# An attention and expert kernel on one core: which engine runs two passes, and which queue loads the first group

## The chip, the core and the metric

The kernel runs on one core of a Trainium2 chip. A core has five engines with an instruction queue each, taken in order: TensorE (PE: matrix products and transposes, with its weight loads shown apart as PEld), VectorE (DVE), ScalarE (ACT), GpSimd (POOL) and SyncE (SP, which here only issues transfers). Transfers between the chip's main memory and the on-chip memory are issued by SP or ACT and run beside the engines. The metric is the device time of one execution in microseconds.

## What is computed

`x` has 4 batches of 11456 rows with 128 columns. Two steps follow one another, all in float32.

```python
def mab(q, kv):
    s = scale * (q @ kv.transpose(0, 2, 1))
    s = s - s.max(-1, keepdims=True)
    a = np.exp(s)
    a /= a.sum(-1, keepdims=True) + 1e-09
    return a @ kv
h = mab(I, x)                 # I: 32 inducing points, so h is 32 rows a batch
return mab(x, h)              # every row of x attends to those 32 rows
```

The result goes through a mixture of experts: a row with `x @ w_skip > 0` takes the best of 8 experts by `x @ w_gate`, and adds `gate * (relu(x @ w1[e]) @ w2[e])` to itself; the others stay as they are. Because every row after the attention is a mean of 32 rows of `h`, the kernel does the expert's work on those 32 rows once a batch, with the weights of one expert, and the gates row by row; a last part (`others`) checks whether any row would have needed another expert.

## The kernel before, in words

The host hands `x` over transposed, so a batch is a tile of 128 partitions (the columns of x) by 11456. A batch is cut into six **groups**: five of 2048 rows of x and one of 1216, which comes first in batch 0 and last in the others. A group is four **quarters** side by side, so that four products of 32 partitions fill the 128.

`first` (lines 348 to 438) handles a group's part in `h`: PE makes the scores (L361), DVE their maximum (L366, L371), ACT the exponentials (L375), PE transposes x and the exponentials (L400, L384), ACT or DVE copies these out of the accumulator banks (L324 or L326), PE sums (L410), DVE adds up (L419). `middle` closes a batch: `h`, the expert, its weights.

`second` (lines 637 to 824) handles a group's rows against `h`. PE makes scores (L659), DVE transposes them back into rows (L664) and finds each row's maximum (L666). Then come three passes of equal shape, each one two-input operation over the whole tile of 128 x 512 (128 x 320 in the short group): `less` subtracts the maximum (L670), `norm` multiplies by one over the sum (L682), and `scale2` multiplies by the row's gate (L786) into a tile `v`. Between them ACT takes the exponential (L673) and DVE sums (L677); DVE transposes the results of norm and of scale2 (both L687) for the closing products of PE (L837). `emit` copies those out (tile `o`) and stores them.

Nobody writes the order down. Each piece is an `Op` with the engines it may run on and a guessed cost on each (`pool(W)`, `dve(W)`, `act(W)`, lines 307 to 317). `in_order` (L65) plays the pieces through a small model of engines and buffers and gives each to the engine that it expects to be done first; `best_order` (L140) draws 1200 changes of the ranks from a fixed seed and keeps those that end no later by this model. A piece that may run on two engines has a `spare` of its own (L55), by which DVE is held back, and which is drawn again too (L162). So a change in what may run where alters every draw behind it, and with it the order of the whole program. The chosen pieces are then issued one after another; each engine runs its own in that order.

`load` (L330) brings a group's columns in. For the very first group (`k == 0`) the cut is at the quarters, so four transfers of 128 x 304; for the others it is in the middle. All are issued by SP. ACT issues two small transfers at the start: the inducing points (`iT_sb`, L219) and the gate weights (L222); and it scales `iT_sb` (L220).

Of the kernel before, what the change touches and what calls it, by code (L numbers as in the profile page):

```python
# [173 lines left out]
def kernel(  # L174
# [9 lines left out]
    nc = tc.nc  # L184
# [122 lines left out]
    def pe(w):  # L307
        return {"PE": 0.1 + 0.9 * w / 512}

    def dve(w):  # L310
        return {"DVE": 0.17 + 0.53 * w / 512}

    def act(w):
        return {"ACT": 0.22 + 0.37 * w / 512}

    def pool(w):
        return {"POOL": 0.1 + 0.95 * w / 512}
# [12 lines left out]
    def load(k, after):  # L330
        b, g = divmod(k, NG)
        s = bt[b]
        G = s.groups[g]
        st = Steps(k)
        buf = s.xbuf[g] = Buf("x")
        cut = G.s1[1:] if k == 0 else [GC // 2]
        cut = [0] + [c for c in cut if c < G.cols] + [G.cols]

        def go(o):
            t = s.x[g] = xp.tile([P, GC], F32, tag="x", name=f"x_{b}_{g}")  # L340
            for c, d in zip(cut, cut[1:]):
                nc.sync.dma_start(out=t[:, c:d], in_=xT[b, :, G.col0 + c:G.col0 + d])

        s.xin[g] = st.add({"SP": 0.08 * len(cut)}, go, after, take=[buf], size=G.cols * 0.512)
        return st
# [291 lines left out]
    def second(s, G, x, main):  # L637


        b, g = s.b, G.g  # L640
        W, nb, nh = G.w2, G.nb, G.nh
        st = {}
        keep = main is None
        L = Steps(b * NG + g + LEAD)
        bs, bl, be, blt = Buf("ps"), Buf("ps"), Buf("e"), Buf("lt")
# [4 lines left out]
        bex = Buf("ex")  # L650
# [33 lines left out]
        def back(k, src):  # L684
            if k == 2:
                st["u2"] = wk.tile([P, GC // Q], F32, tag="u2", bufs=BUFS["u2"], name=f"u2_{b}_{g}")
            nc.vector.transpose(out=st[f"u{k}"][:, 0:W], in_=st[src][:, 0:W])  # L687
# [100 lines left out]
        o = L.add(pe(W), scores, s.o_hc, last["s2"], take=[bs, be, st["b1"]], free=[s.xbuf[g]] if keep else [])  # L788
        last["s2"] = o if keep else None
        o = L.add({"DVE": 2 * dve(W)["DVE"]}, tokens, o, free=[bs])  # L790
        o = L.add({**pool(W), **dve(W)}, less, o)
        o = L.add(act(W), exps, o, take=[bex])
        o = L.add({"DVE": dve(W)["DVE"] + 0.28}, total, o)
        s.o_total.append(o)
        o_v = L.add({**pool(W), **dve(W)}, norm, o, free=[bex])
        st["o1"] = o = L.add(dve(W), lambda o: back(1, "e"), o_v)
        if keep and G.quarters:
            o = L.add({"PE": 0.35}, logits_q, o, s.o_lrq, take=[bl, blt])
            o_m = L.add({"DVE": 0.58}, relative_q, o, free=[bl])
            o_x = L.add({"ACT": 0.6}, gexp_q, o_m)  # L800
            o_c = L.add({"POOL": 1.06}, claim_q, o_m)
            s.o_claim.append(o_c)
            o = L.add({"DVE": 0.54}, gate_q, o_x)
            o = L.add({"POOL": 0.36}, pick_q, o, o_c)
            bm = Buf("ps")
            o = L.add({"PE": 0.35}, to_streams, o, take=[bm])
            o = L.add({"ACT": 0.24, "DVE": 0.17}, gates_in, o, free=[bm])
            o = L.add({**pool(W), **dve(W)}, scale2, o, take=[bv], free=[be, blt])
            st["o2"] = L.add(dve(W), lambda o: back(2, "v2"), o, take=[st["b2"]], free=[bv])
            return st, L  # L810
        o = L.add({"PE": 0.3 + 0.8 * W / 512}, logits, o, s.o_lr, take=[bl, blt])
        o_m = L.add({"DVE": dve(W / 2)["DVE"] + 0.29}, relative, o, free=[bl])
        o = L.add({"POOL": 0.4}, gless, o_m)
        o_x = L.add({"ACT": 0.31}, gexp, o)
        if keep:
            o_c = L.add({"POOL": 0.73}, claim, o_m)
            s.o_claim.append(o_c)
            o = L.add({"DVE": 0.55}, gate, o_x)
            o = L.add({"POOL": 0.2}, pick, o, o_c)
        else:  # L820
            o = L.add({"DVE": 2.0}, lambda o: main(st, lv, gv, two), o_x)
        o = L.add({**pool(W), **dve(W)}, scale2, o, take=[bv], free=[be, blt])
        st["o2"] = L.add(dve(W), lambda o: back(2, "v2"), o, take=[st["b2"]], free=[bv])
        return st, L

# [142 lines left out]
    def other_group(s, gr, w2s, sgn, code, same, G, col0):  # L968
# [5 lines left out]
        def gates(st, lv, gv, two):  # L974
# [22 lines left out]
            nc.vector.tensor_tensor(out=two(gm), in0=two(own), in1=two(sm), op=ALU.mult)  # L997

        st, steps = second(s, G, lambda: x, gates)
        for i, buf in enumerate(st["bufs"]):  # L1000
            buf.idx = i if buf.tag == "ps" else 0
# [20 lines left out]
    def all_steps():  # L1022
        ops = []
        starts = []
        for b, s in enumerate(bt):
            s.xbuf, s.xin, s.first_score = {}, {}, {}
            s.lastm = s.laste = s.lastd = None
            for g in range(NG):
                k = b * NG + g
                ops += load(k, starts[k - AHEAD] if k >= AHEAD else None)  # L1030
                ops += first(s, g)
                starts.append(s.first_score[g])
            ops += middle(s)
            for g, G in enumerate(s.groups):
                st, L = second(s, G, lambda s=s, g=g: s.x[g], None)
                emit(s, G, st, L)
                ops += L
            ops += marking(s, (b + 1) * NG + LEAD + 1)
        return ops + judge(B * NG + LEAD)
# [45 lines left out]
```

## Time and profile before

| | |
|---|---|
| median of 3 runs | 236.57 us (235.46 to 236.66) |
| the profiled execution | 235.9 us, its span from first to last instruction 234.0 us |
| PE, DVE, ACT, POOL busy | 205.8, 178.4, 141.9, 101.4 us |
| mean granted clock of TensorE | 0.966 |

A row of a group view names line, engine, operation, output and inputs, how often, then the busy time in us, the mean of one in ns, and the idle time of the engine before it with what ended it. A row of the view by stretches gives the stretch, its length, the busy time and count of PE, PEld, DVE, ACT and POOL, the granted clock, the share of the transfer engines and GB/s. A busy PE is not PE at its peak: ends of matmuls are modelled.

### The profile page before, as it was taken

Reading aid. Unit: us, or ns where it says so; the run is one execution under the profiler, and the core shown is the slowest. Engines: PE = TensorE matmul, PEld = TensorE weight load, DVE = VectorE, ACT = ScalarE, POOL = GpSimd, SP = SyncE. Lnnn points to the kernel's source line nnn. Section 1 sums busy time; section 2 is a strip of 40 time slices with the busy share of each in tenths; the row PEclk is TensorE's granted clock in tenths of the full one; section 3 lists DMA queues with packets and bytes.
Section 4 is the critical chain, followed back from the end, with each engine's and each line's share of the span. In section 5 each row is a group of like instructions: output and inputs, shape, how many; then the busy total and the mean of one; then the engine's idle time right before and its main releaser. Section 6 shows DMA issues by size and latency. Waiting matters only on the chain.

```text
span 234.0 us, 6690 instructions
## 1 busy us (share of the span) xinstructions
PE 205.8 (88%) x2541; PEld 117.7 (50%) x2542; DVE 178.4 (76%) x484; ACT 141.9 (61%) x326; POOL 101.4 (43%) x231
## 2 busy tenths in 40 slices
PE   4999999999899999998899999899998996869700
PEld 1667776675446754357534565564554332324400
DVE  3244256789888898799899887989998999998510
ACT  2377665655678867668657767477759462554710
POOL 6000000236468740137472162162788647988300
PEclk9999999999999999999999999999999999897975
DMA  6999960760898409995099957600405794161970
GB/s 176 372 418 408 407 235 2 279 263 3 294 347 296 179 4 291 354 417 202 3 349 274 368 197 233 235 3 1 182 4 209 257 372 172 44 263 54 388 265 10
DMA packets 16617, 51.66 MB, mean 221 GB/s; under 512 B 1984, under 2 KB 4928, under 8 KB 16576
## 3 DMA queue, kind: packets, MB, share of 16 engines
q1 hardware_dynamic: 16288, 51.12, 58.9%
q8 instruction: 22, 0.36, 0.6%
q14 instruction: 19, 0.16, 0.2%
q10 hardware_dynamic: 288, 0.02, 0.1%
HBM read 27.68 MB, written 23.46 MB: 219 GB/s over the span
## 4 chain that ended last, share of the span: by engine, by line
PE 55%; DVE 28%; POOL 5%; ACT 4%; issue 4%; DVEq 0%; ACTq 0%; POOLq 0%
PE bank L400 13%; PE bank L837 12%; PE bank L361 8%; PE bank L659 5%; PE bank L410 5%; DVE u L687 4%; PE bank L384 4%; DVE ts L666 3%; DVE ng L366 2%; DVE sums L677 2%; DVE e L664 2%; POOL v L786 1%; PE bank L696 1%; POOL e L682 1%; ACT o L324 1%
## 5 line engine op out<-in xcount | busy, mean ns | idle before, releaser
L324 ACT COPY o<-bank 128x512 f32<-128x512 f32 (+1 forms) x93 | 45.8, 570 | 21.4 <-PE bank L837 17.0
L324 ACT COPY xt<-bank 128x512 f32<-128x512 f32 (+1 forms) x79 | 43.4, 593 | 16.7 <-PE bank L400 16.6
L400 PE MATMUL bank<-ident,x 128*128 128x128 f32 (+1 forms) x368 | 51.6, 284 | 0.4 <-DVE lr L541 0.2
L400 PEld LDWEIGHTS bank<-ident,x 128*128 128x128 f32 (+1 forms) x368 | 40.4, 142 | 13.2 <-issue 3.3
L670 POOL TENSOR_TENSOR e<-e,ts 128x512 f32<-128x512 f32 (+1 forms) x21 | 21.0, 1002 | 58.4 <-DVE ts L666 57.9
L682 POOL TENSOR_TENSOR e<-texp,ts 128x512 f32<-128x512 f32 (+1 forms) x22 | 22.1, 1004 | 31.0 <-DVE ts L679 11.6
L837 PE MATMUL bank<-u,hr 32*128 32x512 f32 (+1 forms) x192 | 27.7, 649 | 1.5 <-ACT o L324 1.5
L410 PE MATMUL bank<-xt,a1T 128*32 128x129 f32 (+1 forms) x736 | 25.1, 275 | 0.3 <-ACT o L324 0.3
L361 PE MATMUL bank<-x,iT_sb 128*32 128x512 f32 (+1 forms) x192 | 25.4, 583 | 0.0
L366 DVE TENSOR_REDUCE ng<-bank 128x1 f32<-128x512 f32 (+1 forms) x24 | 15.3, 637 | 13.0 <-PE bank L361 12.2
L837 PE MATMUL bank<-u,yr 32*128 32x512 f32 (+1 forms) x192 | 24.6, 582 | 0.3 <-DVE u L687 0.3
L659 PE MATMUL bank<-x,hc 128*32 128x512 f32 (+1 forms) x192 | 23.6, 573 | 0.0
L786 POOL TENSOR_TENSOR v<-e,gs 128x512 f32<-128x512 f32 (+1 forms) x21 | 21.0, 1002 | 5.6 <-ACT gs L324 3.1
L410 PEld LDWEIGHTS bank<-xt,a1T 128*32 128x32 f32 (+1 forms) x736 | 19.5, 109 | 5.9 <-issue 2.2
L673 ACT ACTIVATE texp<-e 128x512 f32<-128x512 f32 (+1 forms) x24 | 14.7, 610 | 12.5 <-POOL e L670 8.7
L375 ACT ACTIVATE a<-bank,bias 128x512 f32<-128x512 f32 (+1 forms) x20 | 13.4, 670 | 10.7 <-DVE bias L371 8.7
L687 DVE STREAM_TRANSPOSE u<-e 128x512 f32<-128x512 f32 (+1 forms) x24 | 16.0, 666 | 1.4 <-POOL e L682 1.3
L384 PE MATMUL bank<-ident,a 128*128 128x128 f32 (+1 forms) x92 | 15.1, 286 | 1.6 <-DVE acc L419 1.3
L664 DVE STREAM_TRANSPOSE e<-bank 128x512 f32<-128x512 f32 (+1 forms) x24 | 15.8, 658 | 0.8 <-PE bank L659 0.8
L687 DVE STREAM_TRANSPOSE u<-v 128x512 f32<-128x512 f32 (+1 forms) x24 | 15.9, 665 | 0.7 <-POOL v L786 0.4
L666 DVE TENSOR_REDUCE ts<-e 128x16 f32<-128x512 f32 (+1 forms) x24 | 15.7, 653 | 0.8
L677 DVE TENSOR_REDUCE sums<-texp 128x16 f32<-128x528 f32 (+1 forms) x24 | 15.5, 646 | 0.7 <-ACT texp L673 0.7
(147 smaller groups left out, 280.2 us busy)
## 6 DMA issues: line engine op xcount, KB each, us to landing
x<-in_xT_dram SPq DMA_DIRECT2D x43, 512.0 KB, 7.8
out_dram<-o SPq DMA_DIRECT2D x40, 512.0 KB, 3.6
out_dram<-o SPq DMA_DIRECT2D x8, 304.0 KB, 3.4
w1s<-in_w_dram SPq DMA_DIRECT2D x4, 512.0 KB, 3.7
w2s<-in_w_dram SPq DMA_DIRECT2D x4, 512.0 KB, 5.5
x<-in_xT_dram SPq DMA_DIRECT2D x4, 152.0 KB, 3.1
x<-in_xT_dram SPq DMA_DIRECT2D x3, 96.0 KB, 5.7
iT_sb<-in_iT_dram ACTq DMA_DIRECT2D x1, 16.0 KB, 2.2
```

The source lines that it names most:

```text
L324: nc.scalar.copy(out=out, in_=in_)
L361: nc.tensor.matmul(ps[q * M:(q + 1) * M, 0:W], lhsT=iT_sb, rhs=s.x[g][:, G.s1[q]:G.s1[q] + W], start=True, stop=True)
L384: nc.tensor.transpose(out=pa[0:w, i * P:(i + 1) * P], in_=st["a"][:, c:c + w], identity=ident)
L400: nc.tensor.transpose(out=px[0:w, q * P:(q + 1) * P], in_=s.x[g][:, o:o + w], identity=ident)
L410: nc.tensor.matmul(ph[q * M:(q + 1) * M, 0:P + 1], lhsT=st["aT"][0:w, i, q * M:(q + 1) * M], rhs=xts[bx.idx][0:w, i, q, :], start=(i == 0) ...
L659: nc.tensor.matmul(ps[q * M:(q + 1) * M, 0:W], lhsT=s.hc[:, 0:M], rhs=x()[:, G.s2[q]:G.s2[q] + W], start=True, stop=True)
L666: nc.vector.tensor_reduce(out=mx[:, 0:nb], in_=blocks(t), axis=AX.X, op=ALU.max)
L670: on(o).tensor_tensor(out=blocks(t), in0=blocks(t), in1=wide(st["mx"]), op=ALU.subtract)
L682: on(o).tensor_tensor(out=blocks(st["e"]), in0=ev(M), in1=wide(st["i"]), op=ALU.mult)
L687: nc.vector.transpose(out=st[f"u{k}"][:, 0:W], in_=st[src][:, 0:W])
L786: on(o).tensor_tensor(out=blocks(u), in0=blocks(st["e"]), in1=wide(st["gm"]), op=ALU.mult)
L837: nc.tensor.matmul(bank(bp[q].idx)[:, 0:G.w1], lhsT=m[r, :], rhs=st[k][r, c], start=(k == "u1"), stop=(k == "u2"))
```

## The change

Of the three passes, `norm` and `scale2` may run on POOL alone; `less` still may run on POOL or DVE. The second and fourth quarter of the very first group are issued by ACT instead of SP.

```diff
 def load(k, after):
@@
-            for c, d in zip(cut, cut[1:]):
-                nc.sync.dma_start(out=t[:, c:d], in_=xT[b, :, G.col0 + c:G.col0 + d])
+            for i, (c, d) in enumerate(zip(cut, cut[1:])):
+                (nc.scalar if k == 0 and i % 2 else nc.sync).dma_start(out=t[:, c:d], in_=xT[b, :, G.col0 + c:G.col0 + d])
@@ def second(s, G, x, main):
-        o_v = L.add({**pool(W), **dve(W)}, norm, o, free=[bex])
+        o_v = L.add(pool(W), norm, o, free=[bex])
@@
-            o = L.add({**pool(W), **dve(W)}, scale2, o, take=[bv], free=[be, blt])
+            o = L.add(pool(W), scale2, o, take=[bv], free=[be, blt])
@@
-        o = L.add({**pool(W), **dve(W)}, scale2, o, take=[bv], free=[be, blt])
+        o = L.add(pool(W), scale2, o, take=[bv], free=[be, blt])
```

What the order of the instructions becomes is shown at three places.

The start on ACT (`x_0` is the first group's tile, `xt` and `a_0_0` are what first copies and computes of it); a row with + is new:

```order
 L220 ACT_TABLE_LOAD
 L220 ACTIVATE iT_sb<-iT_sb 128x32
+L342 DMA x_0_184<-in_xT_dram 128x304 x2
 L324 COPY xt_164<-bank_76 128x4x128
 L375 ACTIVATE a_0_0_198<-bank_77,ng_0_207 128x304
```

The two transfers stand behind the scaling of `iT_sb`, and on SP two of the four are gone ahead of the second group's. PE's and DVE's rows for this group are the same in both.

The middle, in batch 1 (`v_1_1` is scale2's output for the second group of batch 1, `gs` its gates). Before, on DVE:

```order
L371 TENSOR_TENSOR bias_5_1854<-ng_5_1852,bias_4_1627 128x1
L326 COPY gs_2_163<-bank_72 128x16
L326 COPY gs_0_153<-bank_76 128x16
L786 TENSOR_TENSOR v_1_1_1871<-e_1_1_1527,gs_0_153 128x512
L687 STREAM_TRANSPOSE u_1_1_1879<-v_1_1_1871 128x512
L460 TENSOR_REDUCE mn_1889<-bank_73 1x32
```

Now, on POOL:

```order
L772 TENSOR_TENSOR lt_5_1422<-lt_5_1422,gs_2_162 128x64
L772 TENSOR_TENSOR lt_1_1515<-lt_1_1515,gs_0_152 128x64
L786 TENSOR_TENSOR v_0_5_1593<-e_0_5_1132,gs_2_163 128x512
L786 TENSOR_TENSOR v_1_1_1617<-e_1_1_1372,gs_0_153 128x512
L760 TENSOR_SCALAR posm<-lt_0_1585 128x16
```

The pass has moved to POOL's queue, behind another group's, and stands earlier among the groups.

The end (`v_3_5` is the last group's scale2; `lo`, `lod`, `lon` and `marks` belong to the check for other experts). Before, on DVE:

```order
L895 TENSOR_REDUCE marks<-gxs 128x1
L786 TENSOR_TENSOR v_3_5_3200<-e_3_5_3007,gs_2_163 128x320
L687 STREAM_TRANSPOSE u_3_5_3203<-v_3_5_3200 128x320
L882 TENSOR_SCALAR lod_3208<-bank_71 128x1
L885 TENSOR_TENSOR lon_3210<-gmax,lod_3208 128x8
L886 TENSOR_TENSOR lon_3210<-lon_3210,gabs 128x8
L887 TENSOR_REDUCE marks<-lon_3210 128x1
L326 COPY o_5_0_3225<-bank_70 128x304
```

Now, on DVE:

```order
L895 TENSOR_REDUCE marks<-gxs 128x1
L882 TENSOR_SCALAR lod_3202<-bank_76 128x1
L885 TENSOR_TENSOR lon_3204<-gmax,lod_3202 128x8
L886 TENSOR_TENSOR lon_3204<-lon_3204,gabs 128x8
L887 TENSOR_REDUCE marks<-lon_3204 128x1
L687 STREAM_TRANSPOSE u_3_5_3209<-v_3_5_3200 128x320
L917 TENSOR_SCALAR two<-bank_76 128x8
```

The pass is gone to POOL, the transpose that reads it stands behind the check's steps, and the copy of the last output is ACT's.

Over the whole program DVE has the passes less, norm and scale2 three, two and three times before, and two, none and none now; of the 72, POOL has the rest.

## The prediction

> **What bounds the kernel now.** I read the page first, then the chain of waits, the stretches of the span, and the places that the change touches.
>
> ```profile
> span 234.0 us, 6690 instructions
> PE 205.8 (88%) x2541; PEld 117.7 (50%) x2542; DVE 178.4 (76%) x484; ACT 141.9 (61%) x326; POOL 101.4 (43%) x231
> PE 55%; DVE 28%; POOL 5%; ACT 4%; issue 4%; DVEq 0%; ACTq 0%; POOLq 0%
> ```
>
> The third line is the chain that ended last: TensorE holds 55% of it and VectorE (DVE) 28%. Where each holds it stands in the view by stretches (length; then PE, PEld, DVE, ACT, POOL busy):
>
> ```profile
> 10.00:30.00 20.00, 20.00 (x280) 14.33 (x279) 7.96 (x18) 12.63 (x28) 0.00 (x0) 1.00 1.03 411
> 82.00:99.00 17.00, 16.32 (x202) 8.19 (x202) 14.79 (x46) 11.94 (x28) 3.71 (x5) 1.00 0.65 213
> 99.00:126.00 27.00, 24.97 (x336) 14.26 (x331) 24.66 (x56) 17.58 (x40) 14.58 (x29) 1.00 0.66 246
> 160.00:180.00 20.00, 19.32 (x283) 10.64 (x279) 18.48 (x52) 15.18 (x40) 13.28 (x29) 1.00 0.25 99
> 190.00:210.00 20.00, 14.67 (x155) 5.75 (x154) 19.12 (x48) 9.08 (x20) 15.03 (x27) 0.91 0.49 192
> ```
>
> From 10 to 30 us PE never idles: whatever starts late there ends late. In the second to fourth stretch PE and DVE are both nearly full; PE idles 0.68, 2.03 and 0.68 us, 3.4 in all, and that is what a lighter DVE could give back there. From 190 on DVE holds the chain (19.12 of 20).
>
> **Part one: the first group's loads.** Rows of the start (start, duration; SPq and ACTq are the engines issuing a transfer):
>
> ```profile
> 0.77 0.41 SPq L342 DMA_DIRECT2D x<-in_xT_dram  x1
> 1.18 0.45 ACTq L222 DMA_DIRECT2D ws_sb<-in_ws_dram  x1
> 3.03 0.23 ACT L220 ACTIVATE iT_sb<-iT_sb 128x32 f32<-128x32 f32 x1
> 4.26 2.59 PE L361 MATMUL bank<-x,iT_sb 128*32 128x304 f32 x8
> 5.62 0.18 PEld L361 LDWEIGHTS bank<-x,iT_sb 128*32 128x32 f32 x2 [0.18 <-DMA x<-in_xT_dram]
> 6.78 2.82 PE L400 MATMUL bank<-ident,x 128*128 128x128 f32 x12
> ```
>
> Before, SP issues the four quarters back to back, and the fourth has landed when its weight load runs at 5.62. After, the second and fourth stand in ACT's order behind the scaling of iT_sb, which ends at 3.26: the order of the program, not the trace, puts them there. At 0.45 us an issue, the fourth leaves at about 3.7, while SP has begun on the big loads.
>
> ```profile
> x<-in_xT_dram SPq DMA_DIRECT2D x43, 512.0 KB, 7.8
> DMA to landing us min/median/max: 2.4/7.0/9.8
> 1.00:2.00 1.00, 0.39 (x1) 0.10 (x1) 0.47 (x1) 0.34 (x1) 0.96 (x12) 1.00 0.15 29
> 2.00:3.00 1.00, 0.00 (x0) 0.00 (x0) 1.00 (x1) 0.95 (x1) 1.00 (x6) 1.00 0.95 261
> 0.00:4.50 4.50, 1.36 (x5) 0.80 (x8) 2.10 (x3) 1.52 (x3) 3.84 (x38) 1.00 0.58 145
> 5.00:6.00 1.00, 1.00 (x5) 0.36 (x4) 0.00 (x0) 0.00 (x0) 0.00 (x0) 1.00 0.93 332
> ```
>
> The second line holds the twelve x loads issued up to 8 us. Lower bound: 2.4 us, the quickest, so 6.1, or +0.5. Upper bound: ACT's pieces wait as those behind SP's backlog do, 7.8 us, so 11.5, or +5.9. Between them, by sharing: by 4.5 us 145 x 4.5 = 652 KB had moved, which is the first group's 623 KB and the small loads; the last quarter was seen at 5.62, some 1.1 later. The loads issued at 0.77 had moved 29 KB by 2.0; at the next row's 261 GB/s that is 0.1 us of flow, so bytes start 1.1 us after issue, and ACT's start at 4.4. If the queues halve 332 GB/s, 311 KB take 1.9 us: landed at 7.4, +1.8. If the engines take a row from each in turn, ACT's rows of 304 x 4 = 1216 bytes against SP's 4096 get 23%, 76 GB/s: 4.1 us, landed at 9.6, +4.0. Both lie far nearer the lower bound than the upper; I take their middle, 8.5: **+2.9 us**.
>
> The second way is what the Trainium skill states (DMA: Bandwidth & Descriptors, section Queues, rings and completion order): the queues of SP and ACT run on the same 16 engines, and an engine with work on both switches between them packet by packet. By it the sum below would be 1.1 us longer, inside the first case's own range. No row of before shows two loaded queues.
>
> What hides it? Nothing: scores of the first group (L361) need all quarters, the transposes behind them (L400, 2.82 us) stand in the same order in both programs, ACT's copies and DVE's maximum wait for PE, and from 10 us on PE is full. Two x loads further on take the same turn-slot as the late quarters and issue later, but with megabytes queued ahead they cost nothing. What SP saves, 2 x 0.41 us of issue, brings the second group's data sooner; PE does not wait for it.
>
> **Part two: the passes.** Groups by shape (busy, mean ns):
>
> ```profile
> L786 POOL TENSOR_TENSOR v<-e,gs 128x512 f32<-128x512 f32 x18 | 18.9, 1048 | 5.4 <-ACT gs L324 3.1 <-DVE u L687 1.6 <-DVE gs L326 0.2
> L786 POOL TENSOR_TENSOR v<-e,gs 128x320 f32<-128x320 f32 x3 | 2.2, 725 | 0.2
> L786 DVE TENSOR_TENSOR v<-e,gs 128x512 f32<-128x512 f32 x2 | 3.0, 1485 | 0.0
> L786 DVE TENSOR_TENSOR v<-e,gs 128x320 f32<-128x320 f32 x1 | 0.5, 491 | 0.0
> L682 DVE TENSOR_TENSOR e<-texp,ts 128x512 f32<-128x512 f32 x1 | 0.7, 694 | 0.1
> L682 DVE TENSOR_TENSOR e<-texp,ts 128x320 f32<-128x320 f32 x1 | 0.5, 491 | 0.0
> L670 DVE TENSOR_TENSOR e<-e,ts 128x512 f32<-128x512 f32 x2 | 1.4, 692 | 0.1
> ```
>
> Eight of the 72 passes stood on DVE. After, norm (L682) and scale2 (L786) have none there and less (L670) has two, so six move net: DVE loses 2 x 1.485 + 0.491 + 0.694 + 0.491 + 0.692 = 5.3 us, and POOL gains 4 x 1.048 + 2 x 0.725 = 5.6, to some 107 of 234. The planner also ranks everything anew. On the chain of waits stood:
>
> ```profile
> 82.91 1.33 DVE v L786
> 100.97 0.69 DVE e L670
> 122.45 1.57 DVE v L786
> 162.16 0.70 DVE e L682
> ```
>
> That is 4.3 us at most, if nothing follows. But each dependent now waits 1.05 us for POOL, and PE has only 3.4 idle us in these stretches. I take half of the 2.03 us in the DVE-led stretch from 99 and 0.3 of the 0.68 from 160: **-1.3** (bounds -3.4 and 0).
>
> Why did the two cost 1.5 and not 0.69? Both engines' rows at that time:
>
> ```profile
> 122.42 1.05 POOL L786 TENSOR_TENSOR v<-e,gs 128x512 f32<-128x512 f32 x1 [0.18 <-DVE gs L326]
> 122.45 1.56 DVE L786 TENSOR_TENSOR v<-e,gs 128x512 f32<-128x512 f32 x1
> L371 DVE TENSOR_TENSOR bias<-ng,bias 128x1 f32<-128x1 f32 x16 | 4.7, 292 | 0.5
> ```
>
> DVE began while POOL ran and ended 0.54 us after POOL's end: it was held.
>
> **The end.** The last group's scale2 moves to POOL, and its last copies to ACT:
>
> ```profile
> 220.00 0.21 POOL L731 TENSOR_TENSOR gs<-gs,gs 128x10 f32<-128x10 f32 x1
> 220.25 0.49 DVE L786 TENSOR_TENSOR v<-e,gs 128x320 f32<-128x320 f32 x1
> 222.36 1.04 ACT L324 COPY o<-bank 128x304 f32<-128x304 f32 x3 [0.44 <-ACT o L324]
> 222.42 0.47 DVE L326 COPY o<-bank 128x304 f32<-128x304 f32 x1 [0.49 <-PE bank L837]
> ```
>
> 0.725 - 0.491 = +0.2; a fourth copy in ACT's row at 1.04 / 3 adds +0.35, so +0.6. Against it, DVE's order behind the last batch's signs has the four small marking steps ahead of them and a copy fewer; I count 0.5 of that. **+0.1** (bounds -1.0 and +0.6).
>
> **The new order elsewhere** I take as 0, within 2.3 us either way, the longest single wait of PE:
>
> ```profile
> PE bank L696 <- DVE u L687: 4.6, 2, 2.3
> ```
>
> **Sum:** 2.9 - 1.3 + 0.1 = +1.7. The profiled execution took 235.9 us around its span of 234.0, inside the runs' 235.46 to 236.66; laid on the median of 236.57 the forecast is **238.3 us**.
>
> **Rivals.**
>
> *The relief pays for the start.* Start +1.8 (halved bandwidth), relief -1.3, end -0.4: 236.7, no change. For it: PE and DVE are close to balance after 82. Against it: PE idles little there.
>
> *The relief decides.* Start +0.5, all of PE's 3.4 idle us, end -0.5: 233.2, or 1.4% faster. For it: two of the passes are held to twice their length. It decides if the late quarters land by 6.5.
>
> *POOL becomes the bound, slower still.* In the last stretch quoted POOL has 15.03 of 20 us. Where a moved pass stays on the chain it costs 1.05 for 0.69, six of them 2.1 us; with +2.9 and +0.6 that is 242.2. It decides if POOL's passes wait in line. For it: any two-input operation of DVE may be held, as 122.45 was.
>
> A rule of the Trainium skill (SBUF — State Buffer, section Who interferes with whom) says just that: a DVE instruction with two SBUF inputs and a GpSimd instruction reading SBUF exclude each other for a whole instruction. The trace's 1485 against 694 ns agrees. It speaks against more passes on POOL, since DVE's small two-input steps stay.
>
> **Chances.** Start late, relief partial (238.3; own range 236.9 to 239.8) 0.37; pays for itself 0.28; relief decides 0.21; POOL the bound 0.14. Some 0.5% either way, 1.2 us, can be told from no change. Slower takes 0.32 of the first and the last: 0.46; no change 0.05 and 0.25: 0.30; faster 0.03 and 0.21: 0.24. The range runs from 235.0 to 241.2: it leaves out the far ends of the second and third rival.
>
> **What would show it.** Right: the first group's L361 ends after 8.5 instead of 6.85 us with a wait on the x load of 2 us or more; L786 has no DVE rows; DVE is busy near 173 us, POOL near 107; PE's idle time from 99 to 126 shrinks. Wrong: the last quarter is in by 6.5; PE gets behind POOL rows in its waits; or the re-ranked order moves PE's idle time by more than 2.3 us, which no row of before can foretell.

## The result: 2.1 us slower, and two larger differences behind it

| | before | after |
|---|---|---|
| median of 4 runs each | 236.01 us (234.55 to 236.66) | 238.13 us (237.68 to 239.13) |
| the profiled execution, and its span | 235.9, 234.0 us | 238.04, 236.3 us |

The ratio is 1.0109, with a 95% interval from 1.0064 to 1.0154. Here and below ratios leave out executions that were disturbed; medians hold all, so a ratio can differ a little from the quotient of two medians (here 1.009).

The forecast was 238.3 us, and slower. The size and the sign are right, but the profile shows that two terms of the sum were wrong and made up for each other. From the page of the kernel after, the span, the engines' busy time and the chain that ended last by engine:

```profile
span 236.3 us, 6674 instructions
PE 206.0 (87%) x2541; PEld 116.9 (49%) x2542; DVE 174.5 (74%) x476; ACT 141.9 (60%) x328; POOL 107.2 (45%) x237
PE 52%; DVE 24%; DMA 9%; ACT 5%; issue 4%; POOL 2%; ACTq 0%; SPq 0%; POOLq 0%; DVEq 0%
```

DVE is 3.9 us lighter and POOL 5.8 us heavier; POOL holds 2% of the chain, 5% before. New is DMA with 9%. Where it stands is seen in the timeline of the start (start, duration, in brackets the idle time before and what ended it):

```profile
2.99 0.84 ACTq L342 DMA_DIRECT2D x<-in_xT_dram  x2
5.11 1.22 PE L361 MATMUL bank<-x,iT_sb 128*32 128x304 f32 x2
10.60 0.19 PEld L361 LDWEIGHTS bank<-x,iT_sb 128*32 128x32 f32 x4 [5.31 <-DMA x<-in_xT_dram]
12.31 0.18 PEld L361 LDWEIGHTS bank<-x,iT_sb 128*32 128x32 f32 x2 [1.53 <-DMA x<-in_xT_dram]
12.32 1.22 PE L361 MATMUL bank<-x,iT_sb 128*32 128x304 f32 x2 [0.49 <-DMA x<-in_xT_dram]
```

and in the chain of waits, where it is the longest piece of all:

```profile
3.38 8.90 DMA x<-in_xT_dram
```

The weight load for the last quarter runs at 12.31 us, where before it ran at 5.62. The first group's scores end at 12.32 + 1.22 = 13.54 instead of 4.26 + 2.59 = 6.85: 6.7 us later, not 2.9. The transfers were not idle meanwhile (view by stretches, the columns as before):

```profile
8.00:9.00 1.00, 0.00 (x0) 0.00 (x0) 0.00 (x0) 0.00 (x0) 0.00 (x0) 1.00 1.05 412
99.00:126.00 27.00, 26.33 (x356) 15.72 (x355) 24.63 (x68) 21.58 (x52) 17.94 (x33) 1.00 0.75 271
190.00:210.00 20.00, 16.36 (x180) 6.00 (x172) 18.91 (x46) 10.44 (x22) 14.14 (x23) 1.00 0.53 209
```

At 8 us every compute engine stands still while 412 GB/s come in: the groups that nobody can use yet. The other two rows show the second difference. From 99 to 126 us PE idles 0.67 us where it idled 2.03, and from 190 on it is busy 16.36 of 20 us where it was 14.67, though the work there comes later (the granted clock of that row is 1.00 where it was 0.91, so a part of this may be the clock). So the kernel starts 6.7 us late and ends 2.3 us late (236.3 against 234.0): some 4.4 us come back on the way. In PE's idle time: up to 30 us it is 8.8 us where it was 3.1, and behind that 21.6 where it was 25.1. The passes, by group:

```profile
L786 POOL TENSOR_TENSOR v<-e,gs 128x512 f32<-128x512 f32 x20 | 20.9, 1050 | 8.7 <-ACT gs L324 7.6 <-DVE gs L326 0.5
L670 DVE TENSOR_TENSOR e<-e,ts 128x512 f32<-128x512 f32 x1 | 0.7, 693 | 0.0
L371 DVE TENSOR_TENSOR bias<-ng,bias 128x1 f32<-128x1 f32 x16 | 6.2, 386 | 0.6
L886 DVE TENSOR_TENSOR lon<-lon,gabs 128x8 f32<-128x8 f32 x4 | 0.7, 167 | 0.1
```

scale2 (L786) has left DVE, and of less (L670) one full-sized pass is left there where two stood. A small two-input step of DVE, L371, costs 386 ns instead of 292; another, L886, 167 instead of 565.

### The profile page after: what moved, and what is told of

The parts are those of the page before. It is cut to its first block, busy times and chain, and to the rows that moved or that the text cites. A ratio compares the mean times of both kernels' runs of the same rounds, so it can differ in the third digit from the quotient of the medians.

```text
span 236.3 us, 6674 instructions
## 1 busy us (share of the span) xinstructions
PE 206.0 (87%) x2541; PEld 116.9 (49%) x2542; DVE 174.5 (74%) x476; ACT 141.9 (60%) x328; POOL 107.2 (45%) x237
## 4 chain that ended last, share of the span: by engine, by line
PE 52%; DVE 24%; DMA 9%; ACT 5%; issue 4%; POOL 2%; ACTq 0%; SPq 0%; POOLq 0%; DVEq 0%
PE bank L400 13%; PE bank L837 12%; PE bank L361 7%; PE bank L410 7%; PE bank L384 4%; DMA x<-in_xT_dram 4%; DVE u L687 3%; PE bank L659 3%; ACT o L324 2%; DVE sums L677 2%; DVE e L664 2%; DMA out_dram<-o 2%; DVE ts L666 2%; DMA w1s<-in_w_dram 2%; DVE ng L366 2%
## 5 line engine op out<-in xcount | busy, mean ns | idle before, releaser
L324 ACT COPY xt<-bank 128x512 f32<-128x512 f32 (+1 forms) x79 | 42.9, 592 | 19.0 <-PE bank L400 18.8
L670 POOL TENSOR_TENSOR e<-e,ts 128x512 f32<-128x512 f32 (+1 forms) x22 | 22.1, 1005 | 63.0 <-DVE ts L666 61.5
L682 POOL TENSOR_TENSOR e<-texp,ts 128x512 f32<-128x512 f32 (+1 forms) x24 | 23.9, 996 | 24.1 <-DVE ts L679 13.1
L361 PE MATMUL bank<-x,iT_sb 128*32 128x512 f32 (+1 forms) x192 | 27.5, 600 | 4.8 <-DMA x<-in_xT_dram 4.8
L837 PE MATMUL bank<-u,hr 32*128 32x512 f32 (+1 forms) x192 | 26.8, 628 | 1.4 <-DVE lt L705 0.6
L786 POOL TENSOR_TENSOR v<-e,gs 128x512 f32<-128x512 f32 (+1 forms) x24 | 23.9, 996 | 9.0 <-ACT gs L324 7.6
L837 PEld LDWEIGHTS bank<-u,yr 32*128 32x128 f32 x192 | 9.9, 191 | 11.2 <-issue 5.9
```

Of the source, the lines that this page charges most:

```text
L324: nc.scalar.copy(out=out, in_=in_)
L361: nc.tensor.matmul(ps[q * M:(q + 1) * M, 0:W], lhsT=iT_sb, rhs=s.x[g][:, G.s1[q]:G.s1[q] + W], start=True, stop=True)
L670: on(o).tensor_tensor(out=blocks(t), in0=blocks(t), in1=wide(st["mx"]), op=ALU.subtract)
L682: on(o).tensor_tensor(out=blocks(st["e"]), in0=ev(M), in1=wide(st["i"]), op=ALU.mult)
L786: on(o).tensor_tensor(out=blocks(u), in0=blocks(st["e"]), in1=wide(st["gm"]), op=ALU.mult)
L837: nc.tensor.matmul(bank(bp[q].idx)[:, 0:G.w1], lhsT=m[r, :], rhs=st[k][r, c], start=(k == "u1"), stop=(k == "u2"))
```

## The experiments

All compare with the kernel before on the same chip. "New order" says whether the program has the order that the planner makes when norm and scale2 may run on POOL alone.

| run | ACT issues quarters | new order | median us | before | ratio, 95% |
|---|---|---|---|---|---|
| passes_alone | no | yes | 231.97 | 235.59 | 0.985 [0.977, 0.993] |
| loads_alone | yes | no | 242.77 | 235.59 | 1.030 [1.020, 1.040] |
| act_early | yes, early | yes | 236.25 | 235.59 | 1.001 [0.996, 1.006] |
| sp_held | yes, SP waits | yes | 233.07 | 235.59 | 0.990 [0.987, 0.994] |
| early_short_rows | yes, early, short rows on SP | yes | 233.51 | 235.28 | 0.987 [0.982, 0.992] |
| moved_only | no | no, passes moved in place | 235.69 | 235.65 | 1.000 [0.997, 1.003] |
| before_draw2, 3, 4 | no | no, other seeds | 234.42, 235.02, 234.24 | 235.69, 235.69, 235.65 | 0.995, 0.996, 0.993 |
| passes_draw2, 3, 4 | no | yes, other seeds | 235.12, 229.86, 231.82 | 235.69, 235.69, 235.65 | 0.994, 0.974, 0.982 |

### The two parts apart

Theory A: two large terms that cancel, the late start and what the passes bring. Theory B: the late start is mostly absorbed on the way, and the passes bring little. One run leaves the loads as before and changes the three lists of engines (both diffs here are against the change):

```diff
-            for i, (c, d) in enumerate(zip(cut, cut[1:])):
-                (nc.scalar if k == 0 and i % 2 else nc.sync).dma_start(...)
+            for c, d in zip(cut, cut[1:]):
+                nc.sync.dma_start(...)
```

> Only norm and scale2 on POOL alone; SP loads all four quarters. Every engine's order is that of the change, two transfers on SP apart. Theory A (two large terms that cancel): the late quarters cost the change what its first scores end later, 13.54 - 6.85 = 6.7 us, and the passes with their new order give back the rest, so this runs 4 to 5 us faster than before, near 231.5 us. Theory B (the late start is mostly absorbed by later slack, and the passes are worth little): within 1.5 us of before, 235 to 237.

The other changes the loads and leaves the lists as before:

```diff
-        o_v = L.add(pool(W), norm, o, free=[bex])
+        o_v = L.add({**pool(W), **dve(W)}, norm, o, free=[bex])
```

(and the same in the two lines of scale2).

> Only the second and fourth quarter on ACT; the passes and every order are those of before. Theory A: 6 to 7 us slower than before, near 242.5 us, with the fourth quarter seen by PE after 11.5 us. Theory B: 1 to 3 us slower, 237 to 239, with the late start visible at 13 us but gone by 100 us.

Measured: 3.6 us faster for the passes alone (231.97 against 235.59), a little less than the 4 to 5 of theory A, and 7.2 us slower for the loads alone (242.77). Theory A holds, and B falls: most of the late start, if not all, reaches the end. The interval of the ratio, 1.020 to 1.040, leaves room for 4.7 to 9.5 us. In the timeline of the loads alone:

```profile
3.40 1.31 ACTq L342 DMA_DIRECT2D x<-in_xT_dram  x2
11.06 0.19 PEld L361 LDWEIGHTS bank<-x,iT_sb 128*32 128x32 f32 x4 [6.62 <-DMA x<-in_xT_dram]
12.77 0.18 PEld L361 LDWEIGHTS bank<-x,iT_sb 128*32 128x32 f32 x2 [1.52 <-DMA x<-in_xT_dram]
```

The last quarter is used at 12.77, 7.15 us after before's 5.62, and the time is 7.2 us longer: as near as the runs can tell, the lateness goes through one to one. With the passes alone the start is before's (timeline):

```profile
5.45 0.18 PEld L361 LDWEIGHTS bank<-x,iT_sb 128*32 128x32 f32 x2 [0.17 <-DMA x<-in_xT_dram]
```

and its span is 230.2 us.

### Why the quarters land so late

Three theories. A1: ACT issues them too late, behind its table load and the scaling of iT_sb. A2: ACT's queue is served behind SP's whenever both have work. A third: transfers of ACT's queue are slow in themselves. One run issues the four quarters ahead of the scaling, with the rest as in the change:

```diff
-    nc.scalar.mul(out=iT_sb, in_=iT_sb, mul=scale)
+    for i in range(Q):
+        (nc.scalar if i % 2 else nc.sync).dma_start(out=x00[:, i * w00:(i + 1) * w00], in_=...)
+    nc.scalar.mul(out=iT_sb, in_=iT_sb, mul=scale)
```

> The change, with ACT's two quarters issued ahead of its table load and the scaling of iT_sb; nothing else moves. Theory A1 (what is late is the issue: by 3.0 us SP's queue has megabytes ahead): the fourth quarter is seen by 6.5 us and the time is that of the passes alone within 1 us. Theory A2 (ACT's queue is served behind SP's whenever both have work): ACT's quarters land after 9 us again and the time stays within 1.5 us of the change, 237 to 239.5.

The other lets SP wait for the first group before it goes on, by a transfer of one column that reads the last quarter:

```diff
+            if k == 0:
+                held = wk.tile([P, 1], F32, tag="held", bufs=1, name="held")
+                nc.sync.dma_start(out=held, in_=t[:, G.cols - 1:G.cols])
```

> The change, with SP's further loads held back until the fourth quarter has landed (a one-column transfer that reads it, ahead of them in SP's queue); ACT issues as late as in the change. Theory A1 and A2 both put the delay on the megabytes of SP: without them the quarters land within 3.3 us of issue, by 6.7 us, and the first scores end by 8; the second group's data then come late, at 10 to 12 us, so 2 to 5 us faster than the change. A third theory (transfers issued by ACT are slow in themselves): they land after 9 us again, and with SP held behind them the time is 3 us or more above the change.

The timeline with the early issue (lines are shifted by 7, L368 is the scores' line):

```profile
1.69 0.94 ACTq L225 DMA_DIRECT2D x<-in_xT_dram  x2
7.91 0.19 PEld L368 LDWEIGHTS bank<-x,iT_sb 128*32 128x32 f32 x4 [3.48 <-DMA x<-in_xT_dram]
9.60 0.18 PEld L368 LDWEIGHTS bank<-x,iT_sb 128*32 128x32 f32 x2 [1.50 <-DMA x<-in_xT_dram]
```

And with SP held (L364 is the scores' line, L345 the one-column transfer):

```profile
3.33 0.45 ACTq L342 DMA_DIRECT2D x<-in_xT_dram  x1
5.75 0.18 PEld L364 LDWEIGHTS bank<-x,iT_sb 128*32 128x32 f32 x2 [0.34 <-DMA x<-in_xT_dram]
5.72 0.54 SPq L345 DMA_DIRECT2D held<-x  x1
```

The issues of ACT's two quarters (KB each, median us from issue to landing), in the change and with SP held:

```profile
x<-in_xT_dram ACTq DMA_DIRECT2D x2, 152.0 KB, 8.2
```

```profile
x<-in_xT_dram ACTq DMA_DIRECT2D x2, 152.0 KB, 2.3
```

The third theory falls: with SP held a quarter lands in 2.3 us, and the last is used at 5.75, 0.13 us after before's. It was issued at 3.33, like the change's, so A1 is not enough either: issued 1.3 us earlier, the quarters are used 2.7 us earlier, but still 4 us later than before. What delays them is SP's loads of 512 KB. But A2 does not say how much, and its range of time (237 and more) was missed by 0.75 us.

The trace holds the start and size of each packet of the transfers; a packet there is one row of a transfer. Counted from the first packet of x (some 1.8 us into the span), for the 256 packets of the quarters on ACT's queue:

```
run               first packet  bytes of SP's 512 KB   while ACT's first 200 went     while all 256 went             last packet
                  of ACT, us    loads gone by then     SP packets   ACT's GB/s        SP packets   ACT's GB/s        ended, us
after             4.91          1.01 MB                242          79                408          63                9.84
loads_alone       5.54          1.09 MB                229          81                392          65                10.34
act_early         1.57          0.05 MB                215          66                383          55                7.19
sp_held           2.09          0                      0            229               0            209               3.58
early_short_rows  1.39          0.01 MB                223          126               451          108               4.26
```

Two things add up. **What was issued ahead goes first.** From the timeline of the change:

```profile
1.71 0.91 SPq L342 DMA_DIRECT2D x<-in_xT_dram  x2
2.98 0.33 SPq L342 DMA_DIRECT2D x<-in_xT_dram  x1
2.99 0.35 ACTq L342 DMA_DIRECT2D x<-in_xT_dram  x1
```

SP issued the two halves of the second group, 1.05 MB, from 1.71 us on, ahead of ACT's first at 2.99, and ACT's first packet leaves when 1.01 MB of them are gone. The two quarters that SP had issued before went ahead too: in all five runs at least 253 of their 256 packets had started before ACT's first, also in act_early, where almost nothing else stood ahead.

**Then packets take turns**: for the first 200 packets of ACT (1216 bytes, a row of a quarter) some 215 to 242 of SP go (4096 bytes, a row of a half), so ACT gets 79 of 401 GB/s in the change. The last 56 come more slowly, with 163 to 168 of SP's long rows; over all 256 ACT gets 63 of 407 GB/s, 16%. So A2 in its strict form, SP always first, falls as well. Why the end of it drags is open: the records do not say which of the 16 transfer engines took a packet. The Trainium skill has the rule that the prediction weighed (DMA: Bandwidth & Descriptors, section Queues, rings and completion order): an engine switches packet by packet between queues. The counts of the first 200 agree with that. But its packet is typically some 9 to 17 descriptors, not one row, and whether an engine changed over after one row or after several is not shown here; that what was issued ahead goes first is not in the rule.

This was found in traces already at hand, so a last run tests the turns on a case that was not: the early issue, with SP's loads of the second and third group cut into rows of 1024 bytes. Theory P is turns by packet, theory C a fixed small share for ACT's queue.

```diff
+            ways = list(range(0, G.cols + 1, 256)) if k in (1, 2) else cut
-            for c, d in zip(cut, cut[1:]):
+            for c, d in zip(ways, ways[1:]):
```

> As the run with ACT's quarters issued early, but SP's loads of the second and third group are cut into eight pieces of 256 columns (rows of 1024 bytes) instead of two of 1024 columns (rows of 4096). The order on all engines is unchanged. The trace's single packets show for the run with early quarters that ACT's first packet went 1.8 us after its issue, and that from then on ACT's packets of 1216 bytes took turns with SP's of 4096: 311 KB out of some 1.2 MB in 5.6 us. Theory P (what was issued earlier goes first, then the queues take turns packet for packet, whatever the packets' sizes): ACT's share becomes 1216 / (1216 + 1024) = 54%; at 300 to 400 GB/s its 311 KB take 1.4 to 1.9 us instead of 5.6, so the last weight load of the first scores runs near 6.0 (5.6 to 6.8) instead of 9.60, and the time falls by about 3 us, to 233 (ratio 0.985 to 0.992). Theory C (ACT's queue gets a fixed small share of the bytes while SP has loads waiting, whatever the packets' size): the last weight load stays near 9.6 and the time at 236.3 (ratio 1.00). A third way: SP's sixteen issues for four cost it so much that the third group comes late; then the first scores are early and the time doesn't follow.

(The expectation's 1.2 MB in 5.6 us is too small: by the packets it is 1.57 MB of SP and 0.31 of ACT.) Its timeline (L369 is the scores' line), and a stretch while the short rows come in, there and in act_early:

```profile
5.82 0.19 PEld L369 LDWEIGHTS bank<-x,iT_sb 128*32 128x32 f32 x4 [1.39 <-DMA x<-in_xT_dram]
6.55 0.18 PEld L369 LDWEIGHTS bank<-x,iT_sb 128*32 128x32 f32 x2 [0.54 <-DMA x<-in_xT_dram]
```

```profile
4.00:5.00 1.00, 1.00 (x4) 0.21 (x3) 0.29 (x1) 0.19 (x1) 0.61 (x8) 1.00 0.96 303
4.00:5.00 1.00, 1.00 (x4) 0.21 (x3) 0.29 (x1) 0.19 (x1) 0.61 (x8) 1.00 0.90 298
```

The last weight load runs at 6.55 (theory P: 5.6 to 6.8; C: 9.6), and the ratio of 0.987 lies within P's 0.985 to 0.992. The turns stayed near one to one over the first 200 (223 of SP), so ACT's share rose to 52%; over all 256 it is 39%, where act_early has 16%. Theory C, a fixed share, falls. ACT's own rate rose less, to 126 GB/s and not P's 160 and more. The short rows are not what keeps it down: in the stretch shown 303 GB/s came in, and 298 with the long rows of act_early.

### Where the passes' gain comes from

Theory R: fewer passes on DVE pay, since DVE and PE are both nearly full. Theory L: the planner's order is a draw, and the change got a luckier one. Three other seeds for each:

```diff
-    rng = random.Random(1)
+    rng = random.Random(2)
```

(3 and 4 in the others; the "passes" kernels have the lists of passes_alone as well.)

> The kernel before, with the planner's 1200 draws from another seed (2 for 1): all passes still free to run on DVE. Theory R (fewer passes on DVE is what pays): within 1.5 us of before, and 2.5 us or more above the same draw with the passes on POOL alone. Theory L (the new order was a lucky draw): it differs from before by 2 us or more one way or the other, and the draws with and without the passes on DVE overlap.

> Norm and scale2 on POOL alone, SP loads all quarters, seed 2. Theory R: 231 to 233.5 us, 2.5 us or more under before_draw2. Theory L: anywhere from 231 to 238.

> The kernel before, seed 3. Theory R: within 1.5 us of before. Theory L: 2 us or more away from it, either way.

> Norm and scale2 on POOL alone, SP loads all quarters, seed 3. Theory R: 231 to 233.5 us. Theory L: anywhere from 231 to 238.

> The kernel before, seed 4. Draws 1 to 3 lay at 1, 0.995 and 0.996 of before. Theory R and L: 0.99 to 1.005 of before.

> Norm and scale2 on POOL alone, SP loads all quarters, seed 4. Draws 1 to 3 lay at 0.985, 0.994 and 0.974 of before. Theory R (a mean gain of 1 to 1.5%, with the draw scattering it by 1%): 0.975 to 0.99, below before_draw4. Theory L: at before_draw4 or above.

Counting the seed of before, the four ratios of the free kernels are 1, 0.995, 0.996 and 0.993, mean 0.996; those with norm and scale2 on POOL alone are 0.985, 0.994, 0.974 and 0.982, mean 0.984. So before has the worst of its four draws, by 0.4% of their mean. Seed by seed the restriction is worth 1.5, 0.1, 2.2 and 1.0%, on the mean 1.2%, some 2.9 us; but four such differences give an interval of about 1.4% either way (an estimate from their scatter), so a gain on the mean is likely and not shown. Both theories missed bounds: L put the free kernels of seeds 2 and 3 at 2 us or more from before, and they lie 1.3 and 0.7 from it; R put passes_draw2 at 231 to 233.5 us, where 235.12 was measured. The third seed gives the best kernel of this study, 229.86 us, ratio 0.974 [0.966, 0.982], ahead of both kernels compared.

R says more than that: that it is DVE's lighter load that pays. One run tests it alone. It keeps before's order and places, and gives norm and scale2 to POOL where they stood on DVE (five of them):

```diff
-            on(o).tensor_tensor(out=blocks(u), in0=blocks(st["e"]), in1=wide(st["gm"]), op=ALU.mult)
+            nc.gpsimd.tensor_tensor(out=blocks(u), in0=blocks(st["e"]), in1=wide(st["gm"]), op=ALU.mult)
```

> The kernel before with its own plan kept on every engine, but the five norm and scale2 passes that stood on DVE issued to POOL at the same places of the program; no new ranks. DVE loses 4.6 us, POOL gains 4.6. Theory R: 2 to 4 us faster than before (231.5 to 233.5). Theory L (the new ranks are what pays, not the move): within 1 us of before or slower, since POOL is in the chain where the plan meant DVE.

Its busy times, the stretch from 99 us, and two groups:

```profile
PE 206.8 (88%) x2541; PEld 117.5 (50%) x2542; DVE 174.8 (74%) x479; ACT 141.9 (60%) x326; POOL 105.9 (45%) x236
```

```profile
99.00:126.00 27.00, 24.96 (x335) 14.56 (x334) 23.90 (x57) 18.19 (x42) 15.58 (x30) 1.00 0.64 239
```

```profile
L371 DVE TENSOR_TENSOR bias<-ng,bias 128x1 f32<-128x1 f32 x16 | 4.7, 292 | 0.5
L886 DVE TENSOR_TENSOR lon<-lon,gabs 128x8 f32<-128x8 f32 x4 | 2.3, 566 | 0.1
```

DVE is 3.6 us lighter, nearly as in the change, and the time is the same: ratio 1.000 [0.997, 1.003]. PE idles 2.04 us from 99 to 126, as before. In passes_alone, whose DVE is busy for 173.1 us, the same stretch is

```profile
99.00:126.00 27.00, 26.75 (x391) 14.43 (x384) 22.57 (x57) 21.07 (x53) 18.80 (x38) 1.00 0.64 237
```

with 0.25 us of idle PE. So the work taken off DVE brings nothing by itself: in the chain of moved_only DVE falls from 28 to 20%, but POOL rises from 5 to 8% and transfers stand in it with 3%. The seeds say the same: passes_draw2 and passes_draw3 both have 169.9 us on DVE and lie 5.3 us apart, and the free kernel of seed 4, with 170.1, takes 234.24. The gain comes with the order that the planner makes. Whether its orders under the restriction are better on the mean, and why, is open.

## Why the prediction came out right, and where it was wrong

**The start, +2.9: wrong by more than half.** Measured are +6.7 us at the first scores, +7.2 in the time alone, and some +6.1 in the whole change (1.0109 - 0.9849 = 2.6% of 236). The last weight load at 12.31 lies outside its upper bound of 11.5. Three steps of it can be told apart now.
- The prediction let ACT's bytes start at 4.4 us. They started at some 1.8 + 4.9 = 6.7, though ACT issued from 2.99 on, no later than counted: 1.01 MB issued ahead by SP went first. This step failed: the prediction asked how two queues share, and did not count what one had in flight when the other began. Its upper bound had the wait, 7.8 us from issue to landing as behind SP's backlog, near the 8.2 measured; it was set aside for the two ways of sharing.
- The way "row by row", with 23% for ACT, is near what the packets show: 20% over the first 200, 16% over all. It gave 9.6 for the landing; with a start 2.3 us later and 4.9 us for the bytes instead of 4.1 it gives 12.7, near the 12.3 seen.
- The other way, halved bandwidth, took part in the middle and does not occur here. The Trainium skill's rule on packets gave the sum 1.1 us more; it was the better of the two, and still short by the wait.

**Nothing hides it: right.** The time of the loads alone grew by 7.2 us (4.7 to 9.5) for 7.15 us at the start. The megabytes queued on SP stood in this part too, but only as a reason why later loads cost nothing; they were what the quarters waited for.

**The relief, -1.3: its reason fell.** DVE's busy time came to 174.5 and POOL's to 107.2, as listed (173 and 107), and PE's idle time from 99 to 126 shrank from 2.03 to 0.67. All the signs of the theory were seen, and it was still not the cause: with DVE just as light in the old order the time did not move (0, within 0.7 us). DVE lost 3.9 us and not 5.3; the 1.5 us more of L371 and the 1.6 less of L886 cancel, and 0.85 us is one copy at the start (L232), which took 2.80 us for 1.95 in this execution and 1.94 in passes_alone.

**The new order, 0 within 2.3: the step that mattered.** It was treated as noise. With the end, which was not timed apart, it carries the passes' whole gain, -3.6 us here, and in the four pairs of seeds -3.6, about 0, -5.2 and -2.4 us, beyond its bounds in three of four. The prediction had named a shift of PE's idle time by more than 2.3 us as a sign of being wrong: behind the first 30 us it is 3.5 us less in the change, 2.0 less in passes_alone, and 0.3 more in moved_only.

**The end, +0.1:** not tested by itself.

**The sum.** +1.7 was forecast; +2.1 was measured by the medians and +2.6 by the ratio, from which the parts are taken. The start was short by about 3.2 us (6.1 - 2.9), the passes with the order and the end by 2.4 (3.6 - 1.2), with opposite signs. That the time was right was luck: two errors of this size cancelled, and the working gave neither.

**The rivals.** POOL as the bound: not seen, POOL holds 2% of the chain, and the moved passes wait for their gates (7.6 of L786's 8.7 us), not in line. "The relief decides if the late quarters land by 6.5" gave 233.2; with SP held the last is used at 5.75 and the time is 233.07, so its condition was well put, though for another reason than the relief. The Trainium skill's rule against POOL (SBUF — State Buffer, section Who interferes with whom), that a two-input DVE step and a GpSimd instruction exclude each other, is borne out step by step. Of the 16 steps of L371 in before, 12 start while POOL runs nothing and take 159 to 161 ns; the other 4 start during a pass on POOL and all end 15 or 16 ns after that pass, having taken 595 to 835. In the change 9 meet a step of POOL and end 12 to 17 ns after it; the other 7 take 158 to 161. Of L886's four steps two met a pass before (954 and 972 ns) and none does in the change (166 to 169). In moved_only, with nearly the same load on POOL, the meetings are those of before, 4 and 2, and so are the means. So what is paid goes by which steps meet, not by how much POOL does.

## What to carry to other kernels

Before a small transfer that is needed early moves to another queue, count the bytes that other queues have issued by the time it leaves, and the rows' lengths: here it waited for the first, and then got its share more by packets than by queues. Two changes that are made together are timed apart, or 3.6 us of gain hide under a loss of 6. Where a planner draws the order, a change of its rules is judged over several draws, and against the same work moved in the old order.

## What was unexpected of the hardware

Packets of two queues took turns almost one for one whatever their length (the first 200 beside 215 to 242 with rows of 4096 bytes, beside 223 with rows of 1024), but only after the 1.0 to 1.1 MB that one queue had issued 0.8 to 1.7 us earlier were gone, and with a slower end (the last 56 beside 163 to 228). A small two-input step of DVE that started during a pass on POOL ended 12 to 26 ns behind it, in each of the cases counted above, and took up to some six times what it takes alone (986 ns for 159). A transfer that found nothing else in the queues was through in 2.3 us, the same one behind these loads in 8.2.

The runs of one kernel differ with the granted clock. In the profiled executions it is full up to some 176 to 227 us and then falls to half, for stretches of 3.4 or 6.8 us and at the very end; how many there are differs between executions. Of the 60 executions of before beside passes_alone, before_draw2 and moved_only, 15 with a mean clock of 0.957 to 0.960 have a median of 236.9 us, 22 with 0.969 to 0.975 one of 234.9. So a part of a difference between orders may be the clock: passes_alone was granted 0.976 to 0.982, which by before's slope (148 us for a whole unit of clock) would be an estimated 2 us of its 3.6; but passes_draw3, the fastest, had 0.961 to 0.963, below the 0.966 that is before's middle. Over the four pairs, at equal clock the estimates are -1.5, -2.4, -5.8 and +0.2 us, mean -2.4 for -2.6 between the medians, so the clock moves single pairs by up to 3 us and their mean little. The change itself was granted 0.970 to 0.979; by the same estimate some 1.5 us of its loss is hidden by the clock. What makes it fall can be read from the 14 traces. They hold 33 falls, and in the 3.4 us ahead of each PE was less busy than elsewhere: 26 to 50% ahead of 30 of them, 59, 70 and 79% ahead of three (before's three: 34, 38 and 26%; passes_alone's two: 29 and 48%). Counted in steps of 3.4 us from each trace's first fall, every stretch behind the first 20 us at full clock with PE at 50% or less was followed by a fall. So the falls come behind idle stretches of PE near the end, which the order of the program makes. Why executions of one kernel differ in them is open.
